# An attention and gated feed-forward kernel whose table of work order is replaced

## The chip, the core and the metric

The kernel runs on one core of a Trainium2 chip. The profile names the core's engines: PE is the matrix engine (PEld its weight loads), DVE the vector engine, ACT the scalar engine with the function tables, POOL the general engine, and SP the queue from which this kernel issues all its DMAs. Each engine works through its own list of instructions in the order in which the kernel wrote them, and waits where an instruction needs something that another engine or a DMA has not finished. The metric is the device time of one execution in microseconds (us). A profiled execution also gives a span, from the first to the last instruction.

## The reference, cut to what matters

Queries, keys and values have shape 4 x 8 x 768 x 64 (batch, heads, positions, head width). Scores are taken inside a narrow window and against one summary per block of 32 keys; the result is turned into 3072 x 512 tokens and goes through a gated feed-forward layer with a cosine gate.

```python
k_sum = k.reshape(B, H, nb, block, D).max(axis=3)      # block 32, nb 24
v_sum = v.reshape(B, H, nb, block, D).mean(axis=3)
scores_l = scale * np.matmul(q, k.transpose(0, 1, 3, 2))       # kept where |i - j| < 16
scores_s = scale * np.einsum('bhsd,bhnd->bhsn', q, k_sum) + np.log(block)
a = softmax(concatenate([scores_l_masked, scores_s]))          # 1e-9 added to the sum
attn = np.matmul(a, concatenate([v, v_sum], axis=2))
x = attn.transpose(0, 2, 1, 3).reshape(B * S, H * D)           # 3072 x 512
h = x @ w_in                                                    # 512 -> 2048
out = (h * np.cos(h)) @ w_out                                   # 2048 -> 512
```

## The kernel before, in words

The tokens are cut into eight blocks of 384 (half of one batch entry). In each block the attention is done for four groups, each a pair of heads; the groups are called a, b, c and d, so that `c3` is the third group of block 3. A group loads q, k and v, turns q and k, takes the largest key of every 32 (`ks`), forms scores on PE (`sc`), copies or scales them out of PSUM (`z`), takes maximum, difference, exponential, sum, reciprocal and product (`mx su ex sm iv nm`), turns the result (`tp` on PE, or `pt` on DVE with a trip through DRAM, `po` and `pi`), and multiplies it with v on PE (`va`). The result is split into a high part and a rest (`xh`, `xl`).

The feed-forward layer runs in 128 steps, `s0` to `s127`. A step takes one of 16 slices of 128 hidden columns for one block. Its up product is 12 matmuls of 384 columns (line 705); then come five short operations on ACT and DVE with one tile `t` (turns L715, residue L718, sine L723, gate L727), a high part `gh` (L344 or L346) and a rest `gl` (L350); its down product is 9 matmuls of 512 columns (line 756), 6 with `gh` and 3 with `gl`, added into three banks of PSUM that the block keeps until its last slice. The tiles `t`, `gh` and `gl` have two buffers each. Block 0 is done in two runs, slices 0 to 5 (s0 to s5) and 6 to 15 (s22 to s31), around the whole of block 1 (s6 to s21). The sixteen weight slices are loaded once and worked into the form that the products need, by ACT, DVE and POOL (`w0` to `w15`: `ab cl sh lb fb hi lo`). The sums over v are formed from loads of their own (`v0_0` to `v3_7`), on POOL or DVE.

What sets the order is a table, `ORDER`: a text of 2118 tokens such as `s4.up.5` or `s0.lo.v`. A token names who works, which operation, and behind that the PSUM banks or staging buffers it uses and the engine that does it (a ACT, v DVE, p POOL). The kernel goes through the table once, and every token writes its instructions to the lists of the engines concerned. No scheduler moves them later; so the order of two tokens matters where they share an engine, and the waits follow from the data.

```python
for token in ORDER.split():
    who, what, *args = token.split(".")
    one = whose[who]
    getattr(one, does[type(one)][what])(*(int(a) if a.isdigit() else eng_of[a] for a in args))
```

Of the kernel before, what the change touches and what calls it, by code (L numbers as in the profile page):

```python
# [28 lines left out]
a0.k a0.tk.1.0 a0.tk.0.1 a0.ks.1 a0.ck.1.a d0.ms.2.3 a0.q d0.k d0.tk.1.0 a0.ks.0 c0.k c0.tk.1.4 c0.ck.1.v a0.ck.0.v  # L29
a0.tq.5 a0.cq.v a0.ms.7.6 c0.tk.0.1 b0.k b0.q b0.tk.0.5 b0.ks.0 c0.ks.0 a0.sc a0.z.0.v b0.tk.1.7 b0.ck.0.v c0.ks.1  # L30
b0.ck.1.v a0.z.1.a a0.mx a0.su d0.tk.0.6 v0_1.l v0_1.h.v b0.tq.5 b0.cq.v c0.q c0.tq.4 c0.cq.a c0.ck.0.a c0.ms.4.1
c0.sc a0.ex c0.z.1.a v0_0.l v0_0.h.p v0_0.s.p c0.v v0_1.s.v d0.ks.1 b0.ks.1 d0.ks.0 a0.sm b0.ms.5.1 b0.sc b0.z.0.v
c0.z.0.v a0.iv c0.mx w1.l w1.ab.0 w1.cl.v w1.sh.4.5 w1.lb w1.fb.1 d0.q d0.tq.7 b0.z.1.a d0.ck.0.a d0.cq.a c0.su c0.ex
c0.sm c0.iv a0.v a0.nm d0.ck.1.a d0.sc a0.tp.1.0 a0.tp.0.1 c0.nm c0.tp.0.4 c0.tp.1.5 b0.mx w1.hi.a w1.lo.p w0.l
w0.ab.0 w0.sh.6.7 w0.cl.v w0.lb c0.m d0.z.0.a d0.z.1.a d0.mx a0.cp.1.a d0.su a0.cp.0.a b0.su w2.l w2.ab.0 w2.sh.0.1
a0.m a0.va.2 w0.fb.1 c0.cp.1.a w0.hi.a w0.lo.p c0.cp.0.a c0.va.3 w2.cl.v w2.lb a0.xh.v d0.ex d0.sm c0.xh.v d0.iv d0.nm
b1.q w5.l w5.sh.4.5 w5.ab.0 b0.ex w2.fb.1 w2.hi.a w2.lo.p d0.m a0.xl a1.ms.6.7 b1.tq.0 b1.cq.a d0.tp.1.2 d0.tp.0.1
d0.cp.1.a d0.cp.0.a c1.q c1.tq.0 w5.cl.v b0.sm w5.lb b0.iv c0.xl b0.nm w3.l a1.q a1.tq.2 a1.cq.a a1.sc w3.ab.0 w5.fb.1
w3.sh.1.2 w3.cl.v w3.lb d0.v a1.z.1.a c1.cq.a a1.z.0.a a1.mx a1.su d0.va.3 d0.xh.a d0.xl c1.ms.4.5 c1.sc c1.z.1.v w4.l
w4.ab.0 w5.hi.v w5.lo.p b0.tp.1.0 c1.z.0.a b0.cp.1.a b1.ms.7.6 w4.sh.3.4 w4.cl.v w4.lb c1.mx c1.su w4.fb.0 b0.tp.0.0  # L40
b0.cp.0.a b1.sc b1.z.1.a b0.v d1.q d1.tq.0 b0.m d1.cq.a b0.va.5 b0.xh.a b0.xl d1.ms.0.6 d1.sc d1.z.1.v a1.ex a1.sm
# [902 lines left out]
```

## Time and profile before

| what | us |
|---|---|
| median of three runs | 658.23 (657.37 to 658.73) |
| the profiled execution, its own time | 658.99 |
| its span | 657.2 |
| PE busy | 635.1 |
| DVE busy | 437.0 |
| ACT busy | 316.7 |
| POOL busy | 247.4 |
| first matmul starts at | 4.70 |
| first up product starts at | 55.88 |

The profiled execution took 0.76 us more than the median, and 1.8 us of it lie outside its span. In rows of a timeline or of the chain of waits the first number is the start after the beginning of the span, the second the time taken; `x12` is a count of instructions. Brackets give the idle time of the engine before that row and what ended it. In rows by stretches of time each engine has busy time and, in brackets, its number of instructions; then stand the granted PE clock as a share of full speed, the busy share of the DMA engines and GB/s.

### The profile page before, as it was taken

The numbers are of one execution on the slowest core, as the hardware profiler recorded it, in microseconds if no ns is written. First come the engines' busy times: TensorE is split into PE (matmuls) and PEld (weight loads), VectorE is DVE, ScalarE is ACT, GpSimd is POOL, SyncE is SP. The second block draws the span as 40 slices with busy tenths as digits, with TensorE's granted clock in tenths as the row PEclk, the third lists the DMA queues.
The fourth block names the chain that finished last, engine by engine and source line by source line (L and its number), as shares of the span: only waits on it lengthen the run. The fifth ranks groups of instructions, "written<-read, shape, count | busy, mean of one in ns | idle before, by whom it ended". The sixth has DMA issues, their size and how long they took to land.

```text
span 657.2 us, 13183 instructions
## 1 busy us (share of the span) xinstructions
PE 635.1 (97%) x5141; PEld 562.7 (86%) x5141; DVE 437.0 (67%) x768; ACT 316.7 (48%) x520; POOL 247.4 (38%) x251
## 2 busy tenths in 40 slices
PE   5679999999999999999999999999999999999996
PEld 4568889888988988898898989889898998899995
DVE  4998999868765667766776856487456675634422
ACT  1698876646553552324555534226433553323232
POOL 3778867465424424012342535115321111301021
PEclk9769999999999999999999999999999999999999
DMA  9997554652334434425444433563124232200001
GB/s 224 289 256 214 155 185 150 194 111 44 85 92 136 121 109 110 116 55 120 106 111 109 130 84 96 123 136 100 47 55 129 81 85 66 75 23 17 32 1 48
DMA packets 167157, 72.67 MB, mean 111 GB/s; under 512 B 136824, under 2 KB 155832, under 8 KB 167096
## 3 DMA queue, kind: packets, MB, share of 16 engines
q1 hardware_dynamic: 167096, 71.84, 41.3%
q8 instruction: 40, 0.66, 0.4%
q14 instruction: 21, 0.17, 0.1%
HBM read 53.72 MB, written 15.73 MB: 106 GB/s over the span
## 4 chain that ended last, share of the span: by engine, by line
PE 88%; DVE 4%; DMA 4%; ACT 1%; SPq 1%; issue 1%; POOL 0%; ACTq 0%; DVEq 0%; POOLq 0%
PE banks L756 38%; PE banks L705 38%; PE banks L560 4%; PE banks L661 4%; PE banks L547 2%; DMA late<-in_moe_w_out_dram 1%; PE banks L617 1%; DMA out_dram<-stage 1%; PE banks L506 1%; DMA late<-in_k_dram 1%; DMA kn<-in_v_dram 1%; SPq L484 0%; DVE t L727 0%; DVE gl L350 0%; PE banks L493 0%
## 5 line engine op out<-in xcount | busy, mean ns | idle before, releaser
L705 PE MATMUL banks<-xh,w 128*128 128x384 f32 x1024 | 278.1, 338 | 1.1 <-DVE stage L406 1.1
L756 PE MATMUL banks<-w,gh 128*128 128x512 f32 x768 | 198.7, 394 | 0.5 <-DVE t L727 0.5
L705 PEld LDWEIGHTS banks<-xh,w 128*128 128x128 f32 x1024 | 186.6, 188 | 6.1 <-DVE stage L406 1.7
L705 PE MATMUL banks<-xl,w 128*128 128x384 f32 x512 | 171.7, 335 | 0.0
L756 PEld LDWEIGHTS banks<-w,gh 128*128 128x128 f32 x768 | 142.5, 188 | 29.0 <-DVE t L727 0.8
L350 POOL TENSOR_TENSOR gl<-t,gh 128x384 fp32r<-128x384 f32 x69 | 70.9, 1031 | 226.5 <-ACT gh L344 99.2
L715 ACT ACTIVATE t<-banks 128x384 int32<-128x384 f32 x128 | 61.9, 489 | 156.9 <-PE banks L705 74.2
L718 DVE SCALAR_TENSOR_TENSOR t<-t,banks 128x384 f32<-128x384 int32 x128 | 69.1, 546 | 75.9 <-ACT t L715 75.8
L723 ACT ACTIVATE t<-t 128x384 f32<-128x384 f32 x128 | 66.3, 524 | 91.4 <-DVE t L718 91.0
L756 PE MATMUL banks<-w,gl 128*128 128x512 f32 x384 | 110.1, 394 | 0.0
L727 DVE TENSOR_TENSOR t<-t,banks 128x384 f32<-128x384 f32 x128 | 69.7, 548 | 48.2 <-ACT t L723 47.2
L705 PEld LDWEIGHTS banks<-xl,w 128*128 128x128 f32 x512 | 96.1, 188 | 2.8
L756 PEld LDWEIGHTS banks<-w,gl 128*128 128x128 f32 x384 | 70.9, 188 | 12.8
L584 POOL TENSOR_TENSOR sc<-sc,m 128x720 f32<-128x720 f32 x28 | 41.2, 1474 | 78.4 <-DVE m L579 78.4
L608 POOL TENSOR_TENSOR sc<-sc,r 128x720 f32<-128x720 f32 x28 | 39.8, 1424 | 42.9 <-DVE r L605 42.0
L344 ACT CAST gh<-t 128x384 fp32r<-128x384 f32 x69 | 34.6, 511 | 32.7 <-DVE t L727 27.3
L350 DVE TENSOR_TENSOR gl<-t,gh 128x384 fp32r<-128x384 f32 x59 | 38.5, 656 | 16.3 <-ACT gh L344 12.0
L350 POOL TENSOR_TENSOR w<-stage,w 128x1024 fp32r<-128x1024 f32 x14 | 34.6, 2471 | 12.0 <-ACT w L344 7.0
L560 PEld LDWEIGHTS banks<-kd,qd 64*64 64x64 f32 x1344 | 27.8, 132 | 6.9 <-issue 3.2
L253 POOL TENSOR_TENSOR kn<-kn 96x256 f32<-96x256 f32 (+1 forms) x32 | 20.0, 625 | 32.1 <-DMA kn<-in_v_dram 16.4
L560 PE MATMUL banks<-kd,qd 64*64 64x24 f32 (+1 forms) x1344 | 30.9, 231 | 0.8 <-ACT qd L499 0.6
L600 DVE TENSOR_REDUCE r<-sc 128x6 f32<-128x726 f32 x28 | 25.2, 899 | 8.0 <-ACT sc L597 7.9
(101 smaller groups left out, 607.8 us busy)
## 6 DMA issues: line engine op xcount, KB each, us to landing
pd<-stage SPq DMA_DIRECT2D x22, 384.0 KB
late<-in_moe_w_in_dram SPq DMA_DIRECT2D x16, 512.0 KB
late<-in_moe_w_out_dram SPq DMA_DIRECT2D x16, 512.0 KB
pt<-pd SPq DMA_DIRECT2D x66, 96.0 KB
vn<-in_v_dram SPq DMA_DIRECT2D x52, 120.0 KB
out_dram<-stage SPq DMA_DIRECT2D x23, 256.0 KB
kn<-in_v_dram SPq DMA_DIRECT2D x24, 192.0 KB
qn<-in_q_dram SPq DMA_DIRECT2D x92, 48.0 KB
```

Source lines behind the costliest of these rows:

```text
L344: eng.copy(out=out, in_=in_)
L350: eng.tensor_tensor(out=lo, in0=src, in1=hi.bitcast(F32), op=ALU.subtract)
L560: nc.tensor.matmul(out=self.sp[hh][s * QT : (s + 1) * QT, c, lo : lo + n], lhsT=self.qd[rows, t * QT : (t + 1) * QT], rhs=self.kd[rows, ke ...
L584: nc.gpsimd.tensor_tensor(out=self.sc, in0=self.sc, in1=self.m.unsqueeze(2).broadcast_to([P, U, NK]), op=ALU.subtract)
L608: nc.gpsimd.tensor_tensor(out=self.sc, in0=self.sc, in1=self.r.unsqueeze(2).broadcast_to([P, U, NK]), op=ALU.mult)
L661: nc.tensor.matmul(out=self.xps[rows, t * QT : (t + 1) * QT], lhsT=self.vn[:, t, rows], rhs=self.pt[2 * c + hh][s], start=True, stop=True,)
L705: nc.tensor.matmul(out=self.h, lhsT=w_of(name, self.f)[:, c * P : (c + 1) * P], rhs=x_of(self.blk, part, c), start=n == 0, stop=n == last,)
L715: nc.scalar.activation(out=self.t.bitcast(I32), in_=self.h, func=AF.Copy, scale=1.0 / TWO_PI, bias=0.25)
L718: nc.vector.scalar_tensor_tensor(out=self.t, in0=self.t.bitcast(I32), scalar=-TWO_PI, in1=self.h, op0=ALU.mult, op1=ALU.add)
L723: nc.scalar.activation(out=self.t, in_=self.t, func=AF.Sin, scale=-1.0, bias=-0.5 * math.pi)
L727: nc.vector.tensor_tensor(out=self.t, in0=self.t, in1=self.h, op=ALU.mult)
L756: nc.tensor.matmul(out=self.acc[i], lhsT=g[:, i * P : (i + 1) * P], rhs=w_of(name, self.f), start=self.first and n == 0, stop=self.last an ...
```

## The change

Only the table `ORDER` is replaced. The new one has the same 2118 operations; a note with it says that loads, sums of v and the changes of the matrix engine between up and down products are counted in it as traced. All functions and all sizes stay. Apart from the places of the tokens, their last parts differ: banks, staging buffers, and for some operations the engine.

```diff
 ORDER = """
-a0.k a0.tk.1.0 a0.tk.0.1 a0.ks.1 a0.ck.1.a d0.ms.2.3 a0.q d0.k d0.tk.1.0 a0.ks.0 c0.k c0.tk.1.4 c0.ck.1.v a0.ck.0.v
-a0.tq.5 a0.cq.v a0.ms.7.6 c0.tk.0.1 b0.k b0.q b0.tk.0.5 b0.ks.0 c0.ks.0 a0.sc a0.z.0.v b0.tk.1.7 b0.ck.0.v c0.ks.1
...
-w12.l v1_3.l v1_3.s.v v1_4.l w6.sh.0.1 s8.tu s8.re s7.hi.v s6.dh.2.3.4 s6.dl w6.cl.p w6.lb w6.fb.1 s5.st.1 w11.l s8.si
...
-s7.dl s10.up.0 s11.up.1 s9.hi.a s8.dh s8.dl s9.dh w12.sh.5.6 s10.tu s9.lo.p s11.tu s11.re s11.si s10.re s10.si w6.lo.p
...
+a0.k a0.tk.0.0 a0.ks.0 a0.ms.1.2 a0.tk.1.3 a0.q d0.k d0.tk.0.4 d0.ck.0.a a0.ck.0.a a0.tq.5 c0.k b0.k b0.tk.1.6
+d0.tk.1.0 a0.cq.v a0.ck.1.v b0.ks.1 d0.ks.1 d0.ks.0 c0.tk.0.7 c0.tk.1.5 c0.ks.1 a0.ks.1 b0.ck.1.v c0.ck.0.a b0.tk.0.4
...
+w6.hi.a s8.si s6.dh.0.1.2 s8.ga s8.hi.v s6.dl s7.dh s7.dl s9.re s9.si w12.ab.0 s8.lo.v s9.ga s9.hi.v s9.lo.v s11.tu
...
```

Counted over the table, the engines that do an operation change as follows.

| operation | before | now |
|---|---|---|
| rest of a step, `gl` | 69 POOL, 59 DVE | 55 POOL, 73 DVE |
| high part of a step, `gh` | 69 ACT, 59 DVE | 60 ACT, 68 DVE |
| rest of a weight slice (`w.lo`) | 14 POOL, 2 DVE | 9 POOL, 7 DVE |
| clamp of a weight slice (`w.cl`) | 3 POOL, 13 DVE | 1 POOL, 15 DVE |
| copy of a turned result (`cp`) | 19 ACT, 1 DVE | 16 ACT, 4 DVE |
| taking a block's results (`ta`) | 12 ACT, 12 DVE | 20 ACT, 4 DVE |

Three places follow as the lists of the engines have them. The first is the beginning of PE's list. Here `late` and `kn` and `x` in line 506 are loaded keys that are turned (`late_127` holds those of a and b, `kn` those of d, `x_2` those of c), line 493 turns a query, line 547 puts a mask into two banks, and line 560 is the first score product of a0. Before:

```order
L506 MATMUL banks<-ident,late_127 128x128 x6
L547 MATMUL banks<-mask,ident 128x360 x2
L506 MATMUL banks<-ident,kn 128x128 x3
L506 MATMUL banks<-ident,x_2_137 128x128 x3
L493 MATMUL banks<-ident,late_128 128x128 x3
L547 MATMUL banks<-mask,ident 128x360 x2
L506 MATMUL banks<-ident,x_2_137 128x128 x3
L506 MATMUL banks<-ident,late_127 128x128 x3
L560 MATMUL banks<-kd_99,qd 64x96
```

And now:

```order
L506 MATMUL banks<-ident,late_127 128x128 x3
L547 MATMUL banks<-mask,ident 128x360 x2
L506 MATMUL banks<-ident,late_127 128x128 x3
L506 MATMUL banks<-ident,kn 128x128 x3
L493 MATMUL banks<-ident,late_128 128x128 x3
L506 MATMUL banks<-ident,late_127 128x128 x3
L506 MATMUL banks<-ident,kn 128x128 x3
L506 MATMUL banks<-ident,x_2_137 128x128 x6
L506 MATMUL banks<-ident,late_127 128x128 x3
L560 MATMUL banks<-kd_99,qd 64x96
```

Ahead of a0's first score product stood both halves of the keys of a and c and one half each of b and d; now all eight halves stand there, and the two masks are one. The list of DVE at the same place (line 527 takes the largest keys, `kd_99` to `kd_102` are the turned keys of a to d, lines 346 and 501 copy keys and queries) was before:

```order
L527 TENSOR_REDUCE kd_99<-banks 128x12 x2
L346 COPY kd_101<-banks 128x384
L346 COPY kd_99<-banks 128x384
L501 TENSOR_SCALAR qd<-banks 128x384
L527 TENSOR_REDUCE kd_100<-banks 128x12
L527 TENSOR_REDUCE kd_101<-banks 128x12
L346 COPY sc<-banks 128x3x120
```

and is now:

```order
L527 TENSOR_REDUCE kd_99<-banks 128x12
L501 TENSOR_SCALAR qd<-banks 128x384
L346 COPY kd_99<-banks 128x384
L527 TENSOR_REDUCE kd_100<-banks 128x12
L527 TENSOR_REDUCE kd_102<-banks 128x12 x2
L527 TENSOR_REDUCE kd_101<-banks 128x12
L527 TENSOR_REDUCE kd_99<-banks 128x12
```

The second of a's two reductions, which a0's scores need, has moved behind one of b, both of d and one of c.

The third place is PE's list at the first down product of block 1, of step s6 (weights `w_436` before, `w_433` now; `xh` and `xl` are the two parts of x). Before, the down product of s6 is followed by the up product of another step:

```order
L756 MATMUL banks<-w_436,gh 128x512 x6
L756 MATMUL banks<-w_436,gl 128x512 x3
L705 MATMUL banks<-xh_1_854,w_758 128x384
L705 MATMUL banks<-xl_1_856,w_758 128x384
L705 MATMUL banks<-xh_1_854,w_758 128x384 x2
L705 MATMUL banks<-xl_1_856,w_758 128x384
L705 MATMUL banks<-xh_1_854,w_758 128x384
```

Now four down products stand in one row, and four up products ahead of them:

```order
L705 MATMUL banks<-xh_1_958,w_699 128x384
L756 MATMUL banks<-w_433,gh 128x512 x6
L756 MATMUL banks<-w_433,gl 128x512 x3
L756 MATMUL banks<-w_397,gh 128x512 x6
L756 MATMUL banks<-w_397,gl 128x512 x3
L756 MATMUL banks<-w_462,gh 128x512 x6
L756 MATMUL banks<-w_462,gl 128x512 x3
L756 MATMUL banks<-w_795,gh 128x512 x6
L756 MATMUL banks<-w_795,gl 128x512 x3
L705 MATMUL banks<-xh_1_857,w_1212 128x384
```

Over the whole list of PE, an up product directly follows a down product 71 times before and 11 times now; a down product directly follows an up product 81 times before and 22 times now. The pieces of attention that stand between feed-forward work are 39 before and 38 now. Runs of down products with no up product among them that are longer than four steps are 1 before (five steps) and 9 now (five to eight steps).

More of the change, by code (lines that the diff above doesn't have):

```diff
@@ L34 @@
[L34 to L38, printed above, removed]
@@ L170 @@
+s127.re s127.si s127.ga s127.hi.v s127.lo.p s126.dh s126.dl s127.dh s127.dl s127.ta.2.a s111.st.0 s127.ta.0.0.v
+s127.st.2 s127.st.0 s127.tb.2.v s127.sb.2 s127.ta.1.1.a s127.st.1
 """
```

268 lines of the change are left out of this document (136 added, 132 removed).

## The prediction

> **What bounds the kernel now.** I read the page first, for the busy shares and the slices, then the stretches of time, then the chain of waits and the timeline of PE where it has gaps.
>
> ```profile
> PE 635.1 (97%) x5141; PEld 562.7 (86%) x5141; DVE 437.0 (67%) x768; ACT 316.7 (48%) x520; POOL 247.4 (38%) x251
> PE   5679999999999999999999999999999999999996
> PEclk9769999999999999999999999999999999999999
> ```
>
> PE is busy for 97% of the span; what it is short of lies in the first three slices and the last, and in slices two and three its clock was lowered.
>
> ```profile
> 0.00:56.00 56.00, 40.78 (x585) 31.08 (x586) 44.91 (x64) 33.86 (x52) 36.02 (x55) 0.85 0.95 251
> 56.00:130.00 74.00, 72.92 (x457) 65.37 (x457) 67.88 (x101) 54.47 (x84) 52.57 (x46) 1.00 0.59 177
> 130.00:652.00 522.00, 521.26 (x4102) 466.27 (x4100) 323.61 (x604) 227.53 (x384) 158.82 (x151) 1.00 0.34 86
> 652.00:657.20 5.20, 0.17 (x1) 0.00 (x0) 0.64 (x2) 0.87 (x2) 0.00 (x0) 0.72 0.42 151
> ```
>
> So four stages. Up to the first up product at about 56 us, PE is idle for 56.00 - 40.78 = 15.2 us; from there to 130 us for 1.1; in the 522 us behind for 0.7; at the end for 5.0, in which the last results are taken and stored. Between 56 and 652 us no wait is left to remove that is worth more than 1.8 us in all. There the new order can only gain from how closely matmuls follow each other, and it can lose wherever PE now waits.
>
> **The change part by part.** All 5141 matmuls stay, so the work of PE stays; its order changes.
>
> *Changes between up and down products.* The chain of waits, whose pieces are PE itself here, prices them:
>
> ```profile
> 92.73 2.10 PE banks L705 x12
> 94.84 2.08 PE banks L756 x9
> 96.92 2.10 PE banks L705 x12
> ...
> 408.08 8.34 PE banks L705 x48
> 416.43 6.84 PE banks L756 x30
> 423.27 2.10 PE banks L705 x12
> 425.37 1.39 PE banks L756 x6
> ```
>
> By the starts, 12 up matmuls between down products take 94.84 - 92.73 = 2.11 us and 48 take 8.35. The 36 more cost 6.24, which is 2.08 for 12: an up piece behind a down piece pays 0.03 beside its matmuls. Likewise 9 down matmuls take 2.08 and 30 take 6.84: 21 more cost 4.76, or 0.227 each, so 9 should cost 2.04 and a piece pays 0.04; the piece of 6 took 1.39 against 1.36, or 0.03, and I give a piece of 3 0.02. Up behind down goes from 71 times to 11: 60 x 0.03 = 1.8 us less. Down behind up goes from 81 (10 pieces of 3 matmuls, 12 of 6, 59 longer) to 22 (all of 18 or more): 0.2 + 0.36 + 2.36 = 2.9 before, 0.9 now, 2.0 less. Together 3.8. The starts are rounded to 0.01, which makes each price uncertain by about 0.005: 120 changes by 0.005 are 0.6, so 3.2 to 4.4. I take 3.6, a little under the middle, since the 0.03 for an up piece rests on the smallest difference.
>
> *Pieces of attention* between feed-forward work cost something too:
>
> ```profile
> 448.25 1.02 PE banks L560 x36
> 449.27 2.29 PE banks L705 x12
> 451.55 2.08 PE banks L756 x9
> ```
>
> Behind scores 12 up matmuls took 451.55 - 449.27 = 2.28, or 0.17 over 2.11. There are 39 such pieces before and 38 now; one fewer is 0.2 us at most, and I leave it out.
>
> *The beginning.* PE's rows up to its last large wait:
>
> ```profile
> 6.01 2.61 PE L547 MATMUL banks<-mask,ident 128*128 128x360 f32 x4
> ...
> 9.79 1.38 PE L547 MATMUL banks<-mask,ident 128*128 128x360 f32 x4
> ...
> 11.32 0.49 PE L506 MATMUL banks<-ident,late 128*128 128x128 f32 x3
> 11.75 1.09 PE L560 MATMUL banks<-kd,qd 64*64 64x96 f32 x48
> ...
> 22.36 1.08 PE L560 MATMUL banks<-kd,late 64*64 64x24 f32 x46 [1.57 <-DVE kd L527]
> 24.06 0.55 PE L493 MATMUL banks<-ident,qn 128*128 128x128 f32 x3 [0.61 <-DMA qn<-in_q_dram]
> 26.88 2.44 PE L560 MATMUL banks<-kd,late 64*64 64x96 f32 x48 [2.27 <-ACT late L499]
> 29.25 1.54 PE L617 MATMUL banks<-ident,sc 128*120 128x128 f32 x6
> 31.31 1.54 PE L617 MATMUL banks<-ident,late 128*120 128x128 f32 x6 [0.52 <-POOL late L608]
> 33.35 1.55 PE L661 MATMUL banks<-pt,vn 120*64 120x64 f32 x24 [0.51 <-ACT pt L344]
> 37.36 1.55 PE L661 MATMUL banks<-pt,x 120*64 120x64 f32 x24 [2.46 <-ACT pt L344]
> ```
>
> and, from the groups by line, DVE's reduction of keys:
>
> ```profile
> L527 DVE TENSOR_REDUCE kd<-banks 128x12 f32<-128x384 f32 x10 | 5.3, 551 | 4.0 <-ACT kd L344 2.2 <-PE banks L506 1.7
> ```
>
> Now a0's scores stand behind b's keys. Those had landed by 11.32 at the latest, when PE turned them without a wait, and their load is again the fifth. From b's first half on, four groups of three transposes stand up to the last of c, at most 0.43 us each by the step from 11.32 to 11.75, and then DVE's reductions of c and a at 0.55 each: 4 x 0.43 + 2 x 0.55 = 2.8. If b's keys land between 10.5 (an estimate, halfway between the rows at 9.79 and 11.32) and 11.3, a0's scores begin at 13.3 to 14.1 instead of 11.75, 1.5 to 2.4 us late. What this holds up is a0's softmax, and with it the transposes that stood at 29.25. But from 20 to 37.4 us PE waited 1.57 + 0.61 + 2.27 + 0.52 + 0.51 + 2.46 = 7.9 us for DVE, a query, ACT and POOL, so there is room to be late in. Against it, c's query is now loaded ahead of b's and of the second load of v; POOL, and no longer DVE, does the halving of v; and the masks and queries of block 1 (`a1.ms`, `b1.tq`, `a1.tq`) now stand ahead of c0's product with v, where PE waited 2.46 us. Queries for d still come behind the first weight slice, so the wait that ended at 24.06 stays. I take the first up product at the same 56 us, with bounds from 3 us earlier (less than half of the 7.9 us removed) to 5.4 later (the third rival).
>
> The lowered clock belongs here. Four masks took 2.61 us at 6.01 and 1.38 at 9.79, so the rate doubled, and later it fell back:
>
> ```profile
> 9.20:26.30 17.10, 11.23 (x184) 7.86 (x182) 15.78 (x24) 5.44 (x9) 8.37 (x8) 1.00 1.09 270
> 26.30:43.30 17.00, 12.93 (x121) 10.55 (x122) 16.00 (x20) 15.47 (x23) 14.77 (x9) 0.50 0.92 275
> ```
>
> Half the clock held for 17 us behind gaps of 0.6 and 2.27 us. The Trainium skill, "TensorE: Matmul & The Clock Gate", section "Part 1: The HAM clock gate", says that the half rate is the default, and that a busy window of some 3.4 us lifts it and an idle one brings it back. By that rule a start with fewer gaps would run 17 us less at half the clock, and one with a gap ahead of a0's scores would stay at it longer; the trace agrees in the rate, but its longest gap there, 2.27 us, is shorter than such a window, so partly idle windows seem to count. The sum would stay at its value by either, unless the gaps move; that is the third rival.
>
> *Waits in the long runs.* A step's `t` comes free when its rest is done, and there are two. The loop without neighbours, from the end of the program:
>
> ```profile
> 642.02 0.49 ACT L715 ACTIVATE t<-banks 128x384 int32<-128x384 f32 x1 [2.10 <-PE banks L705]
> ...
> 646.03 0.49 ACT L715 ACTIVATE t<-banks 128x384 int32<-128x384 f32 x1 [1.18 <-POOL gl L350]
> ```
>
> 646.03 - 642.02 = 4.01 us for every second step, against two down products of PE, 2 x 2.05 = 4.1. Four steps are ready when a run begins (two with `gh` and `gl`, two with `t`), so runs up to four don't feel the loop; a fifth step and those behind it do, with 0.1 us to spare for two steps, and less where attention's work on ACT or DVE falls between. The run of five at the end of the program went through without a gap. I take no more waits than the 1.8 us of now, and keep 0 to 5.4 as bounds (nine long runs with 0.4 each, that is 3.6, on top of 1.8).
>
> *More work on DVE.* Moving `gl` and weight rests to DVE takes it from 67.88 of 74 us in the second stage:
>
> ```profile
> L350 POOL TENSOR_TENSOR w<-stage,w 128x1024 fp32r<-128x1024 f32 x14 | 34.6, 2471 | 12.0 <-ACT w L344 7.0
> L350 DVE TENSOR_TENSOR w<-stage,w 128x1024 fp32r<-128x1024 f32 x2 | 2.4, 1220 | 0.0
> ```
>
> Five more rests at 1.22 are 6.1 us over the sixteen slices, and as much room is left (74 - 67.9). Up to the 16th gate DVE has 166 instructions before and now, because products with v and sums have gone to ACT and POOL in turn. I cost it at nothing; the room hides it, and without that it is part of the bounds above. The end is the same three takes and four stores in another order, and stays at its 5 us.
>
> *The sum.* From the profiled execution, 658.99 - 3.6 = 655.4 us; that execution lay 0.76 over the median, so the median of the new order should be about 654.6.
>
> **The rivals.**
>
> First, a shorter beginning: PE's waits for ACT and DVE at 22 to 37 us shrink, and with them perhaps the stretch at half the clock. For it speaks that block 1's masks and queries now fill c0's wait and that ACT has three copies of `pt` fewer; against it that d's query and the weights land when they did (DMA engines 0.95 busy to 56 us). 3 us less: 651.6.
>
> Second, the long runs starve: nine places at 0.4 us give back the 3.6, and the time is 658.2. For it speaks the loop of 4.01 against 4.1; against it that five steps in a row ran free at the end.
>
> Third, on the other side, the beginning at half the clock: a0's scores wait behind b's keys, the gap ahead of them keeps the clock low, and the 11.23 us of PE work between 9.2 and 26.3 take twice as long. 22.5 us do not fit into 17.1; the first up product comes 5.4 us later, and the time is 654.6 + 5.4 = 660.0. It decides from a first up product after about 60.8 us (55.9, the 3.6 gained, and 1.3). For it speaks that masks of 2.61 us and transposes of twice the time were the state before 9 us; against it that 5.9 us of the stretch were idle and that other chains go on meanwhile.
>
> Fourth, the price of a change is not saved, because the same cost sits elsewhere, as at the ends of accumulations, which stay: 658.2. Against it speaks that pieces of 48 and 30 contain such ends and don't show it.
>
> **How the numbers follow.** The forecast has a chance of 0.43, the shorter beginning 0.19, starving runs 0.14, the slow beginning 0.16 and no saving 0.08. The likeliest case alone spans 652.5 to 656.8. A measurement of this kernel can tell about 0.2%, or 1.3 us, from no change: faster is under 656.9, slower over 659.5. Faster gets 0.43 + 0.19 = 0.62, the same 0.14 + 0.08 = 0.22, with 0.02 of it given to slower for runs that starve longer: 0.20, and slower 0.18. The range of 650.0 to 660.3 reaches over the first rival and just over the third; left out are a beginning shorter by over 4.6 us and several losses at once, together under 0.2.
>
> **What would show each step right or wrong.** In the new profile's chain, pieces of 36 to 72 up matmuls at 2.08 us for 12 and of 27 or more down matmuls at 0.227 each show the saving; stretches such as 130 to the end of PE's work would be shorter by about 3 us with the same waits. The start of the first up product, 55.88 now, tells the beginning's part directly, with the granted clock of its slices. Gaps ahead of line 756 inside runs, released by `gh` or `gl`, would show starving; gaps ahead of line 705 released by a weight slice would show DVE too full. The forecast is wrong if the first up product moves by over 2 us, or if PE is idle for over 4 us between it and its last matmul.

## The result and the profile after

The new order takes 653.91 us in the median of four runs (653.28 to 655.12), against 658.48 us before (657.37 to 659.19, four runs). The ratio is 0.9935, with an interval from 0.9919 to 0.9951: 4.6 us faster, where 3.6 were forecast. The profiled execution took 654.17 us, with a span of 652.4 against 657.2, so the two traces differ by 4.8 us, and these can be placed.

From the page of the new kernel, the busy times and the granted clock by 40 slices:

```profile
PE 630.4 (97%) x5141; PEld 558.6 (86%) x5141; DVE 450.3 (69%) x797; ACT 304.1 (47%) x503; POOL 216.0 (33%) x234
PEclk9789999999999999999999999999999999999999
```

The same 5141 matmuls keep PE busy 4.7 us less; DVE has 13.3 us more. By stretches of time (columns as before: busy time of PE, PEld, DVE, ACT and POOL, then granted clock, DMA share, GB/s):

```profile
0.00:56.00 56.00, 40.24 (x593) 30.01 (x594) 45.70 (x67) 33.32 (x53) 33.75 (x51) 0.91 0.93 249
56.00:130.00 74.00, 74.00 (x470) 67.56 (x469) 67.29 (x104) 53.48 (x82) 44.66 (x50) 1.00 0.58 177
130.00:647.00 517.00, 515.71 (x4080) 461.01 (x4079) 336.73 (x627) 216.39 (x368) 137.56 (x135) 1.00 0.34 87
647.00:652.40 5.40, 0.40 (x2) 0.00 (x0) 0.62 (x2) 0.87 (x2) 0.00 (x0) 0.78 0.40 146
```

PE waits for 1.29 us between 56 and 647 us (517.00 - 515.71), where it waited for 1.8 before, and for 5.0 at the end, as before. The beginning, by PE's timeline:

```profile
10.72 0.52 PE L506 MATMUL banks<-ident,late 128*128 128x128 f32 x3 [1.64 <-DMA late<-in_k_dram]
...
13.29 1.53 PE L560 MATMUL banks<-kd,qd 64*64 64x96 f32 x48
...
22.31 1.86 PE L560 MATMUL banks<-kd,late 64*64 64x96 f32 x48 [2.35 <-DVE late L501]
...
33.70 1.01 PE L661 MATMUL banks<-pt,vn 120*64 120x64 f32 x24 [2.09 <-DMA vn<-vs]
...
35.94 1.48 PE L547 MATMUL banks<-mask,ident 128*128 128x360 f32 x4 [0.54 <-DVE stage L406]
38.89 0.77 PE L493 MATMUL banks<-ident,late 128*128 128x128 f32 x3 [1.47 <-ACT pt L344]
39.59 1.55 PE L661 MATMUL banks<-pt,x 120*64 120x64 f32 x24
...
44.07 1.38 PE L547 MATMUL banks<-mask,ident 128*128 128x360 f32 x4
...
54.35 0.45 PE L705 MATMUL banks<-xh,w 128*128 128x384 f32 x1
```

The keys of b landed at 10.72 and a0's scores began at 13.29, as forecast; yet the first up product starts at 54.35 instead of 55.81. (The prediction's 55.88 was the end of what stands ahead of it; from here on starts of matmuls are compared.) So 1.5 of the 4.8 us between these two traces come from the beginning. From there to the end of the last matmul it is 593.05 us instead of 596.36, which is the other 3.3.

The two parts don't stand equally firm. The stretch behind the first up product repeats: in four runs below that leave it alone (e3, e7, e8, e9) it is 592.7 to 593.4 us, and in two with the order before (e6, e12) 595.6 and 597.8. The beginning doesn't: four runs below (e1, e2, e5, e11) have the new order's beginning unchanged, and their first up products start at 56.43, 54.34, 54.37 and 54.58. The same lists can thus differ by 2.1 us there, more than the 1.5, which rest on one trace of each kernel.

Long pieces in the chain of waits look as expected:

```profile
240.04 10.42 PE banks L705 x60
250.46 8.20 PE banks L756 x36
```

60 ups take 10.42, or 2.08 for twelve, and 36 downs 0.228 each. The 593 and 596 us can be summed over the steps from one matmul's start to the next. Idle time is counted by itself; of what is left of a step, an up product has 0.1733 us and a down product 0.2267 us, the same sum in both kernels, and what goes beyond that is sorted. Steps that go beyond by 0.08 us or more (by 0.1 us as a rule) are called slow steps.

```
                                                     before   after   difference
first ten matmuls of an up or down piece that
  stands directly behind one of the other kind,
  without slow steps                                  4.42     1.18      -3.24
slow steps at the ends of pieces (75 and 65)          7.86     6.69      -1.17
slow steps inside pieces (0 and 16)                   0.00     2.00      +2.00
PE's idle time                                        1.81     1.29      -0.52
products of attention                                53.88    53.16      -0.72
the rest                                              0.87     1.20      +0.33
together                                                                 -3.3
```

The first row is the price of changes, forecast at 3.6. It is steady: 4.42 and 4.41 in e6 and e12, which have the order before behind the first up product, and 1.16 to 1.18 in e3, e7, e8 and e9, which have the new one.

### The profile page after: what moved, and what is told of

Read it like the earlier page. It is cut to its first block, busy times and chain, and to the rows that moved or that the text cites. A ratio compares the mean times of both kernels' runs of the same rounds, so it can differ in the third digit from the quotient of the medians.

```text
span 652.4 us, 13154 instructions
## 1 busy us (share of the span) xinstructions
PE 630.4 (97%) x5141; PEld 558.6 (86%) x5141; DVE 450.3 (69%) x797; ACT 304.1 (47%) x503; POOL 216.0 (33%) x234
## 4 chain that ended last, share of the span: by engine, by line
PE 88%; DVE 6%; ACT 1%; issue 1%; SPq 1%; POOL 1%; DMA 1%; ACTq 0%; DVEq 0%
PE banks L705 40%; PE banks L756 38%; PE banks L560 4%; PE banks L661 4%; PE banks L617 1%; SPq L447 1%; POOL w L350 1%; DVE kd L527 1%; DMA late<-in_k_dram 1%; PE banks L547 1%; DVE stage L406 1%; DVE vs L263 1%; DVE m L579 1%; DVE t L727 0%; DVE t L718 0%
## 5 line engine op out<-in xcount | busy, mean ns | idle before, releaser
L705 PE MATMUL banks<-xh,w 128*128 128x384 f32 x1024 | 268.6, 337 | 0.1
L350 POOL TENSOR_TENSOR gl<-t,gh 128x384 fp32r<-128x384 f32 x55 | 57.3, 1043 | 223.9 <-DVE gh L346 107.6
L718 DVE SCALAR_TENSOR_TENSOR t<-t,banks 128x384 f32<-128x384 int32 x128 | 69.4, 546 | 67.0 <-ACT t L715 66.3
L584 POOL TENSOR_TENSOR sc<-sc,m 128x720 f32<-128x720 f32 x28 | 39.2, 1403 | 72.4 <-DVE m L579 70.3
L350 DVE TENSOR_TENSOR gl<-t,gh 128x384 fp32r<-128x384 f32 x73 | 45.0, 620 | 16.7 <-ACT gh L344 10.4
L344 ACT CAST gh<-t 128x384 fp32r<-128x384 f32 x60 | 30.7, 511 | 39.5 <-DVE t L727 28.2
L346 DVE CAST gh<-t 128x384 fp32r<-128x384 f32 x68 | 28.3, 417 | 15.7 <-PE banks L756 12.4
L597 ACT ACTIVATE sc<-sc 128x720 f32<-128x720 f32 x28 | 22.5, 805 | 27.4 <-POOL sc L584 27.3
L253 POOL TENSOR_TENSOR kn<-kn 96x256 f32<-96x256 f32 (+1 forms) x36 | 23.3, 647 | 32.0 <-DMA kn<-in_v_dram 23.6
```

Source lines behind the costliest of these rows:

```text
L344: eng.copy(out=out, in_=in_)
L346: eng.tensor_copy(out=out, in_=in_)
L350: eng.tensor_tensor(out=lo, in0=src, in1=hi.bitcast(F32), op=ALU.subtract)
L584: nc.gpsimd.tensor_tensor(out=self.sc, in0=self.sc, in1=self.m.unsqueeze(2).broadcast_to([P, U, NK]), op=ALU.subtract)
L705: nc.tensor.matmul(out=self.h, lhsT=w_of(name, self.f)[:, c * P : (c + 1) * P], rhs=x_of(self.blk, part, c), start=n == 0, stop=n == last,)
L718: nc.vector.scalar_tensor_tensor(out=self.t, in0=self.t.bitcast(I32), scalar=-TWO_PI, in1=self.h, op0=ALU.mult, op1=ALU.add)
```

## The experiments

The kernel before ran again beside each group of experiments, with medians of 658.60 to 659.36 us, and the ratios are against those runs. The new order didn't; times over its 653.91 us are therefore sure to about 1 us only.

**1. Changes put back (e1_alternate).** At 14 places of the new order where a step's 12 up matmuls stand ahead of a step's six early down matmuls, the two alternate, two ups and one down. That adds 140 changes and moves nothing else.

```diff
+        def up_with_down(self, i, d, *banks):
+            ...
+            for n, (c, name, part) in enumerate(ups):
+                nc.tensor.matmul(...)                      # the up product as in up()
+                if n % 2 and n // 2 < len(downs):
+                    d.products([downs[n // 2]])
```

> The changed kernel, in which at 14 places an up product is followed by the first 6 matmuls of a down product; here these 18 matmuls alternate, two of up and one of down. That adds 140 changes between up and down (33 to 173) and no matmul. If every change costs 0.03 to 0.04 us whatever the length of the pieces, as the prediction has it: 140 x 0.035 = 4.9 us more than the changed kernel's 653.9, so about 658.8. If the cost is a slower rhythm of the first six to nine matmuls behind a change (their starts lie 0.176 to 0.181 apart instead of 0.173 for up and 0.231 to 0.236 instead of 0.227 for down): 14 x (12 x 0.005 + 6 x 0.006) = 1.3 us, so about 655.2. If a change costs nothing and the gain came from waits: 653.9.

Measured: 657.05 us (655.85 to 659.00), ratio 0.9972 [0.9957, 0.9987] against before. Its profiled execution had a slower beginning (first up product at 56.43; why, is looked at under 5), so only the stretch from there to the last matmul is compared; by stretches, this kernel and then the new order:

```profile
56.40:652.30 595.90, 593.06 (x4565) 530.88 (x4557) 406.03 (x733) 271.31 (x452) 181.83 (x184) 1.00 0.37 98
```

```profile
54.35:647.40 593.05, 591.76 (x4561) 530.22 (x4557) 405.66 (x733) 271.51 (x451) 182.56 (x184) 1.00 0.37 98
```

PE is idle for 2.84 us in the one and 1.29 in the other. Of 2.75 us by starts (595.80 against 593.05), 1.55 are thus waits, and 1.2 are left for 140 changes: 0.009 each at most. At 0.03 to 0.04 each they would have cost 4.2 to 5.6. Changes that follow each other after one or two matmuls are far cheaper than the prediction's price; whether the price itself fell, this run couldn't say.

**2. The price by itself (e5_price).** Behind the last token stand blocks of matmuls that wait for nothing and whose results nobody uses.

```diff
+            for piece in (48, 24, 12, 6, 3, 1):
+                for n in range(192):
+                    one_down(DM) if n // piece % 2 else one_up(0, self.f)
+            for piece in (48, 6):                          # downs of 384 columns
+                for n in range(192):
+                    one_down(TB) if n // piece % 2 else one_up(0, self.f)
+            for piece in (48, 6):                          # ups only, two banks and slices
+                for n in range(192):
+                    one_up(n // piece % 2, self.f - n // piece % 2)
```

> The new order, and behind its last token matmuls whose results nobody uses: six blocks of 96 up and 96 down products in pieces of 48, 24, 12, 6, 3 and 1 (3, 7, 15, 31, 63 and 191 changes inside a block); then 96 ups and 96 downs of only 384 columns in pieces of 48 and of 6; then 192 ups in pieces of 48 and of 6 that alternate between two banks and two weight slices. Nothing waits inside the blocks, so each block's length tells the price of a change by itself. The base is 96 x 0.1733 + 96 x 0.2267 = 38.40 us. Price of the prediction, 0.03 to 0.04 for each change whatever the piece: 38.5, 38.6, 38.9, 39.5, 40.6 and 45.1 us. A slower rhythm of the first 9 matmuls behind a change (0.004 us each) and nothing else: 38.5, 38.7, 39.0, 39.2, 39.2 and 39.2. If the different widths cause it, the pair of blocks with 384 columns on both sides shows no difference between pieces of 48 and 6, and the last pair neither; if it is the change of tensors or banks, both pairs show one of 0.4 to 1.0.

Measured in its one execution, from the starts of the matmuls: 38.62, 38.67, 38.93, 38.96, 39.15 and 39.04 us for pieces of 48, 24, 12, 6, 3 and 1, and 33.28 in all four of the other blocks. In its chain of waits (L718 the ups, L726 the downs; start, length, matmuls):

```profile
666.99 8.34 PE banks L718 x48
675.33 10.92 PE banks L726 x48
686.26 4.18 PE banks L718 x24
...
724.92 2.10 PE banks L718 x12
727.03 2.76 PE banks L726 x12
729.79 2.10 PE banks L718 x12
...
766.31 1.04 PE banks L718 x6
767.35 1.39 PE banks L726 x6
768.74 1.04 PE banks L718 x6
...
914.28 1.04 PE banks L718 x6
915.32 1.04 PE banks L726 x6
916.36 1.04 PE banks L718 x6
```

A pair of 48 takes 686.26 - 666.99 = 19.27, or 0.07 over 48 x 0.4; a pair of 12 takes 4.87, again 0.07 over 4.80; a pair of 6 takes 2.43, or 0.03 over 2.40. So an isolated pair of changes costs 0.07, which is the prediction's 0.03 + 0.04. But it isn't paid at the change. It is a slower rhythm of the matmuls behind it, by a few ns each up to about the sixth up and the ninth down, so shorter pieces pay only for the matmuls that they have, and 191 changes in single matmuls cost 0.6 us in all, not 5.7 more than none. Downs of 384 columns in pieces of 6 show nothing (914.28 to 916.36 is 2.08 = 12 x 0.1733), nor does a change of bank and weights alone. So here the price hangs on the two widths, 384 and 512 columns. Why a change of width slows the next matmuls, no run shows.

**3. Shorter pieces by later ups (e2_late_ups).** 54 up products of the new order were moved later, one place of many shown by PE's tokens, so that direct changes rise from 33 to 96.

```diff
-... s11.up.6 s9.up.7 s8.up.4 s10.up.3 s6.dh.0.1.2 s6.dl s7.dh s7.dl ...
+... s9.up.7 s8.up.4 s6.dh.0.1.2 s6.dl s11.up.6 s10.up.3 s7.dh s7.dl ...
```

> The changed kernel with part of the grouping undone: 54 up products stand later in PE's list, behind down products, as far as two pieces of PE's work stay between them and their own turns; everything else stays. Direct changes between up and down go from 33 to 96. With the price of the prediction: 33 x 0.03 + 30 x 0.035 = 2.0 us more, so 655.9, and PE's idle time as it was. If the grouping saved waits and no change costs: the pieces keep their time (12 up matmuls 2.08 us, 9 down 2.04) and only idle time grows. If grouping was worth nothing: 653.9.

Measured: 722.2 us (719.8 to 723.7), ratio 1.0954 [1.0927, 1.0981]. By what PE waited for (total, times, longest) between 56 and 717 us:

```profile
PE banks L756 <- DVE gh L346: 9.0, 8, 2.8
...
PE banks L705 <- DVE t L727: 5.0, 4, 1.7
PE banks L756 <- ACT gh L344: 4.7, 1, 4.7
```

Over 40 us of waits, and the mean granted clock from 130 us on fell to 0.97. The theory that pieces differ only by the price of their changes fell by far. An up product that starts early also starts the chain turns, residue, sine, gate, high part that its down product needs. The long pieces of the new order work because each run of ups stands ahead of the run of downs that it feeds.

**4. How near the long runs are to starving (e11_rests_pool).** All 73 rests `gl` on DVE go to POOL.

```diff
-... s1.lo.v ... s2.lo.v ...
+... s1.lo.p ... s2.lo.p ...
```

> The new order with all 128 rests gl on POOL (73 of them were on DVE; 1.02 us each there instead of 0.56). It lengthens the loop by which a tile t comes free by 0.46 us for more than half of the steps. Theory of the prediction, a loop of 4.01 us against 4.1 for two steps leaves 0.1: the long runs of down products starve, by 0.2 to 0.3 us for each of some 20 steps behind the fourth of a run, PE idle 4 to 7 us more between the first up and the last down product, time 3 to 7 over the new order's. Rival, steps are far enough ahead: idle as in the new order (1.3 us), time within 0.7.

Measured: 668.03 us (667.09 to 669.37), ratio 1.0141 [1.0119, 1.0163], 14 us over the new order; from the first up product (54.58) to the last matmul it is 605.74 us, 12.7 more. The direction is that of the prediction's theory, but not the place. From PE's timeline and POOL's:

```profile
119.52 1.65 PE L756 MATMUL banks<-w,gl 128*128 128x512 f32 x3 [4.10 <-POOL gl L350]
```

```profile
115.54 1.24 POOL L253 TENSOR_TENSOR kn<-kn 96x256 f32<-96x256 f32 x2 [2.75 <-DMA kn<-in_v_dram]
...
117.53 1.94 POOL L350 TENSOR_TENSOR gl<-t,gh 128x384 fp32r<-128x384 f32 x2
```

Eight pauses of 0.37 to 4.27 us make 10.6 of the 12.7, all within the first four steps of runs of at most four steps, save one of 0.79 in the third step of the run of eight. The largest is a queue: the rest stands on POOL behind a sum of v that waited 2.75 us for its load. In the other eight long runs no pause is over 0.14 us: in the run of seven that begins at 610.4, the starts of 63 matmuls span 14.09 us, where 62 x 0.2267 = 14.05 are the least. So a rest that takes 0.46 us more doesn't starve a long run, and the prediction's loop, with 0.1 us to spare and a cost from the fifth step on, isn't what limits them. Something else may help the long runs here: DVE is busy for 410.3 us instead of 450.3, so its own parts of the loop come sooner. Why there is more room than the loop at the program's end suggested stays open. What more rests on DVE spare is the queue behind POOL's other work.

**5. What sets the beginning: the clock? (e3_fill, e6_before_fill, e7_after_fill2, e9_after_fill3.)** Idle mask products fill PE's waits, so that the clock stays full. In the new order 23 of them (e3), then eleven in shorter fills (e7, e9); in the order before, six (e6).

```diff
+        def fill(self, i, n):
+            for _ in range(n):
+                nc.tensor.matmul(
+                    out=bank(i)[:, : QC * NK].rearrange("p (c n) -> p c n", c=QC), lhsT=ident,
+                    rhs=mask[:, self.half : self.half + QC, :], start=True, stop=True,
+                )
```

> The changed kernel with 23 added matmuls (identity times mask, into banks that are free, never read) at four places of the beginning where PE waited: ahead of b0's scores, of the first turn of a0's result, of a0's product with v, and of the turn of b1's query. They keep PE busy and change no other work. If the lowered clock (22.0 to 28.8 and 39.1 to 42.5 us) costs: it stays at full, the pieces of PE between them take half (about 4 us less of PE time) and the first up product comes 1 to 2.5 us earlier than 54.35, the time 651.4 to 652.9. If the beginning is set by loads, DVE, ACT and POOL: the clock stays full but the first up product stays within 0.4 us and the time at 653.9. If the fillers come in the way: later than 54.35 by up to 2 us.

> The order before, with three idle mask products ahead of d0's scores and three ahead of c0's product with v, in the two largest waits of PE's beginning (2.27 and 2.46 us); they go to a bank that is overwritten. Theory that before's 17 us at half the clock made its beginning longer: the clock stays full up to c0's product with v at about 37.4, and the 18.45 us of work behind it, of which 5.98 ran at half the clock, shrink by 3.0: first up product at 52.8 to 53.5 instead of 55.81, time 2.3 to 3.0 under before. Rival, the beginning is set by the loads and the weights' preparation, and the clock only fills waits: first up product at 55.5 to 56.5, time within 1 us of before.

> The new order with eleven idle mask products in four waits of PE's beginning (3 ahead of b0's scores, 3 ahead of a0's first turn of weights, 3 ahead of a0's product with v, 2 ahead of the query of a1 that waits for c0), about half as many as in the run with 23, where the fillers outlasted the waits by 1 to 1.6 us. Theory that the clock lengthens the work behind the last wait: from that query on 13.5 us at the full clock instead of 15.5, first up product at 52.4 to 53.2, time 1.2 to 2.0 under the new order's. Rival, loads and other engines set the first up product: 54 to 55, time within 0.7 of the new order's.

> As the run with eleven fillers, but the last two stand ahead of the masks of a1 and in a bank of those masks, so that they wait for nothing that the masks don't wait for (there they had waited 3.29 us for the clamp of a weight slice). Theory that the lowered clock lengthens PE's work behind its last wait: clock full from 9 us on, first up product at 52.4 to 53.4 instead of 54.35, time 1.0 to 2.0 under the new order's 653.9. Rival, the clock costs only what waits hide: first up product at 54.0 to 55.0, time within 0.7 of the new order's.

Measured: e3 654.85 us, ratio 0.9935 [0.9921, 0.9950], first up product at 55.03; e6 658.29, ratio 1.0001 [0.9980, 1.0022], at 56.30; e7 658.44, ratio 0.9998 [0.9983, 1.0014], at 58.25; e9 654.63, ratio 0.9946 [0.9927, 0.9965], at 54.53. In the new order two stretches run at half the clock, and in e9 none does; by stretches, first the new order:

```profile
22.00:28.80 6.80, 4.82 (x57) 3.89 (x57) 6.72 (x11) 3.94 (x6) 3.75 (x3) 0.50 0.89 250
...
39.10:42.40 3.30, 3.16 (x32) 2.44 (x31) 3.01 (x6) 3.17 (x6) 2.24 (x3) 0.50 0.88 235
```

```profile
10.50:56.00 45.50, 38.09 (x596) 27.17 (x595) 44.27 (x62) 31.59 (x50) 29.17 (x17) 1.00 0.97 260
```

What e9 won on PE came back as waits that had been covered; from its timeline:

```profile
40.93 0.62 PE L624 MATMUL banks<-ident,late 128*120 128x128 f32 x4 [0.99 <-DVE late L501]
...
51.85 0.52 PE L493 MATMUL banks<-ident,qn 128*128 128x128 f32 x3 [0.62 <-DMA qn<-in_q_dram]
...
54.53 0.44 PE L712 MATMUL banks<-xh,w 128*128 128x384 f32 x1
```

The clock was full in e9 and the first up product didn't come earlier. In e6 half the clock held for 6.8 us instead of 17, and again nothing was gained. These runs show that filling the waits doesn't pay; they don't show that the lower clock is free, for the fillers stand in PE's list too. In e6 c0's product began at 38.79 instead of 37.36.

e1 tells more. Up to 96 us its lists are those of the new order, and in its trace the wait for `pt` that ended at 38.89 in the new order ended at 38.95. From its timeline behind that:

```profile
41.33 1.59 PE L617 MATMUL banks<-ident,late 128*120 128x128 f32 x6 [0.99 <-DVE late L501]
...
45.33 2.52 PE L547 MATMUL banks<-mask,ident 128*128 128x360 f32 x4
...
56.43 0.44 PE L705 MATMUL banks<-xh,w 128*128 128x384 f32 x1
```

Half the clock held here from 40.81 to 47.64, in the new order's trace from 39.07 to 42.49. The masks that took 1.38 us there took 2.52, and the first up product came 2.1 us later. PE waits for nothing behind 41.33 in either trace, so the clock alone is left to make the difference. Half the clock costs nothing where it only fills a wait: in the new order's trace it took the place of the 0.99 us that PE waits for DVE in e1 and e9. Where no such wait is left, it is paid. How much of the new beginning's 1.5 us is the clock, whose 17 us at half had become 10, these runs don't tell. Over the 70 executions of the kernel before that ran beside the experiments, the clock and the time go together: the 15 with a mean clock of 0.989 or more have a median span of 655.9 us, the 24 with 0.984 or less 658.3. Which of the two follows from the other, or both from a third, that doesn't say.

The Trainium skill, "TensorE: Matmul & The Clock Gate", section "Part 1: The HAM clock gate", says that windows of some 3.4 us decide, and the lengths at half the clock agree (3.41, 6.83 and 17.07 us are one, two and five of them).

In e7 the last two fillers went to a bank that a weight slice still used, and PE waited for DVE:

```profile
40.74 2.77 PE L553 MATMUL banks<-mask,ident 128*128 128x360 f32 x4 [3.29 <-DVE stage L406]
```

The first up product was 3.9 us late, and the time is 4.5 over the new order's. So a delay on PE's list at this place is paid, while a gain there may not be kept.

**6. The order of the beginning (e8_masks_behind, e4_a0first, e12_before_mask_first, e10_two_masks_less).** e8 undoes one part of the change: the masks of a1 and the queries of b1 and a1 stand behind c0's product with v again.

```diff
-... b1.tq.5 d0.nm ... a1.ms.6.7 w2.fb.1 b1.cq.v ... a1.tq.2 a1.cq.a ... c0.va.4 d0.m ...
+... c0.va.4 b1.tq.5 b1.cq.v a1.ms.6.7 a1.tq.2 a1.cq.a d0.m ...
```

> The new order with one part of its beginning undone: the masks of a1 and the queries of b1 and a1 stand behind c0's product with v again, as in the order before. Theory that this move is worth the work it takes out from behind the last wait (1.48 + 0.33 + 0.33 at the full clock): first up product 1.5 to 2.5 later than 54.35, at 55.8 to 56.9, time 1.5 to 2.5 over the new order's. Rival, the beginning's gain is all clock, or is set elsewhere: first up product at 54 to 55, time within 0.7 of the new order's.

Measured: 655.75 us (655.09 to 656.46), ratio 0.9959 [0.9943, 0.9975], 1.8 us over the new order:

```profile
39.04 1.55 PE L661 MATMUL banks<-pt,x 120*64 120x64 f32 x24 [2.25 <-ACT pt L344]
...
41.21 2.61 PE L547 MATMUL banks<-mask,ident 128*128 128x360 f32 x4
...
56.66 0.45 PE L705 MATMUL banks<-xh,w 128*128 128x384 f32 x1
```

c0's product begins half a microsecond earlier than in the new order (39.04 against 39.59), but the masks and queries now stand behind it: first up product at 56.66, 2.3 later than in the new order's trace and 0.85 later than in that of the kernel before. That is the work that was moved, but not alone: half the clock held here until 44.14, and the masks took 2.61 us instead of 1.48. Six executions are 1.6 us slower than the new order by the ratios (0.9959 against 0.9935), at the edge of what the two intervals can tell apart. So this part of the new order is worth 1.6 us by the times and 2.3 by the traces; that the beginning would have become longer without it, one trace doesn't show.

e4 undoes another part: a0's scores stand ahead of b's keys again.

```diff
-... b0.tk.1.6 d0.tk.1.0 ... b0.ks.0 c0.ks.0 a0.sc c0.ms.3.5 ... a0.z.0.a ... a0.mx ...
+... a0.ks.1 a0.sc b0.tk.1.6 d0.tk.1.0 ... c0.ks.1 a0.z.0.a a0.z.1.v a0.mx ...
```

> The changed kernel with a0's scores put back ahead of b's keys on PE, and the largest keys of a, the copies of a0's scores and its maximum moved forward with them on DVE. PE's wait of 1.64 us for b's keys no longer stands ahead of a0's scores, which should start near 9.8 instead of 13.29 us. If that lateness was hidden, as the prediction has it: first up product within 0.5 us of 54.35, time 653.4 to 654.4. If it set the beginning: 1.5 to 2.4 us earlier, 651.5 to 652.4. If the clock stays low longer because PE is now idle elsewhere: later.

Measured: 655.83 us (654.88 to 658.26), ratio 0.9947 [0.9927, 0.9967]. The scores began at 9.58 instead of 13.29, and the first up product came at 56.52. (The traced execution is the slowest of the six, and half the clock held in it from 38.52 to 45.35.) Starting a0's scores 3.7 us earlier gained nothing: none of the six executions is under the new order's median. So what holds them up was rightly called hidden.

e12 does one part alone in the order before: only the masks of a1 go ahead of c0's product with v.

```diff
-... c0.va.3 ... a0.xl a1.ms.6.7 b1.tq.0 ...
+... a1.ms.6.7 c0.va.3 ... a0.xl b1.tq.0 ...
```

> The order before with one thing of the new one: the masks of a1 (2.77 us at half the clock, at 38.85) stand ahead of c0's product with v, in PE's wait of 2.46 us that ended at 37.36. The bank that they need comes free at 35.28, by the second DVE operation L406 of that stretch (34.06 + 1.22), so they fill that wait from there to 38.05, 0.7 over its end. Theory that PE's work behind the wait sets the first up product: 2.77 - 0.69 = 2.1 us earlier, at 53.2 to 54.5 instead of 55.81, time 1.3 to 2.5 under before. Rival, that DVE and the weights set it (as where two masks fell away and half of it came back as waits): first up product earlier by under 1 us or with new waits of 1 us and more right behind it, time within 0.8 of before.

Measured: 660.67 us (657.3 to 662.51), ratio 1.0022 [1.0003, 1.0041], 1.5 over before. The rival's new wait came, but its time missed too.

```profile
35.69 2.77 PE L547 MATMUL banks<-mask,ident 128*128 128x360 f32 x4
38.39 1.06 PE L661 MATMUL banks<-pt,x 120*64 120x64 f32 x24
41.31 0.55 PE L493 MATMUL banks<-ident,late 128*128 128x128 f32 x3 [1.86 <-DVE stage L406]
...
57.79 0.45 PE L705 MATMUL banks<-xh,w 128*128 128x384 f32 x1
```

The masks filled the wait as worked out, but the query behind them (`b1.tq.0`) then waited 1.86 us for DVE: its bank 0 is that of the weight slice `w2.sh.0.1`, and the masks had covered that wait before. Half the clock held for 20.5 us, the last 6.8 of them from 42.16, behind PE's last large wait. In the new table that query has bank 5. So in the order before the move alone doesn't pay, and the bank was in its way; the move with the other bank was not run there.

e10 asks whether less PE work behind the last wait is worth its length: b1 and d1 get their masks from DVE, as the blocks behind do.

```diff
-MASKS = "11111111000000000000000000000000"
+MASKS = "11111010000000000000000000000000"
-... b1.ms.4.3 b1.sc ... b1.z.1.a ... d1.ms.3.4 d1.sc ...
+... b1.sc.4.3 ... b1.z.1.v ... d1.sc.3.4 ...
```

> The new order; for b1 and d1 the mask is no longer put into PSUM by PE but added by DVE when it takes the scores, as the groups of blocks 2 to 7 do it: eight records of mask products (1.31 + 1.41 us by the steps of the timeline) fall away on PE behind its last wait, and one take goes from ACT to DVE (about 0.5 us). Theory that PE's own work behind the last wait sets the first up product: 51.5 to 52.2 instead of 54.35, time 2.0 to 2.9 under the new order's 653.9. Rival, that the weights or DVE (9.6 of 10 us busy there) set it: first up product at 53.8 to 54.9 with a wait of PE in front or right behind, time within 0.7.

Measured: 655.41 us (654.4 to 656.47), ratio 0.9949 [0.9931, 0.9967], no gain over the new order (0.9935 [0.9919, 0.9951]).

```profile
49.90 0.92 PE L661 MATMUL banks<-pt,vn 120*64 120x64 f32 x24 [1.18 <-ACT pt L344]
...
52.88 0.44 PE L705 MATMUL banks<-xh,w 128*128 128x384 f32 x1
...
54.43 0.44 PE L705 MATMUL banks<-xl,w 128*128 128x384 f32 x1 [0.59 <-DVE xl L350]
```

The first up product came 1.47 earlier, half of the 2.7; 1.18 us went into a wait for ACT ahead of it, and from it to the last matmul it is 595.70 us instead of 593.05, with waits for DVE and ACT behind it. From 36 to 76 us DVE is busy for 39.0 of 40 us here, ACT for 34.3 and PE for 33.6, so an earlier first up product isn't by itself an earlier end. Of all orders tried here none was faster than the new one.

## Why the prediction was right, and where it was not

**Time and range.** 653.91 against 654.6, in the range and in the forecast's own range. The profiled execution's 4.8 us are 3.3 in the long stretch and 1.5 in the beginning; the forecast had 3.6 and 0. The 3.3 are borne out by other traces; the 1.5 lie within what the same beginning differs by.

**Changes between up and down products: right, a little over.** The prices held when measured by themselves (0.07 for an isolated pair of changes). In place the slower rhythm fell by 3.24 us, against the 3.6 taken and the bounds of 3.2 to 4.4. That the stretch as a whole gained about as much is in part luck: 2.0 us came back as slow steps inside long pieces, and 1.2 at the ends of pieces, 0.7 in attention and 0.5 of idle time went, none of which the sum had. The fourth rival, no saving, is out. What the prediction didn't see is that the price lies on the matmuls behind a change: it multiplied a price by a count, which holds here since nearly all pieces were long enough to pay in full, and fails in e1.

**Waits in the long runs: right in size, not in the loop behind it.** 1.29 us, where no more than 1.8 was taken. The five largest pauses inside pieces are 0.44 to 0.22 us, four of them waits for `gh` or `gl`; half of the 2.0 us of slow steps stand beside these four. The second rival's nine times 0.4 didn't come, though a smaller cost of its kind did. But the reason given for their bounds, a loop of `t` with 0.1 us to spare from the fifth step on, fell: with all rests on POOL eight of the nine long runs went through with no pause over 0.14 us (e11).

**DVE: right.** Between 56 and 130 us it was busy for 67.29 of 74 us, and PE waited for nothing there. The room wasn't needed: of the 6.1 us that were to fill it nothing shows in this stretch, where 67.88 stood before; the 13.3 us more lie behind it.

**The beginning: taken as unchanged, shorter by 1.5.** The forecast of a0's scores (13.3 to 14.1) held at 13.29, and that their delay is hidden was borne out by e4. The weak step is the sum at its end, "I take the first up product at the same 56 us": it named the masks and queries that fill c0's wait, but didn't price them. Undoing that part costs 1.6 us by the times of e8 and 2.3 at its first up product, some of it by the clock. The 1.5 that remain in the two traces are less than the 2.1 by which the same beginning differed in e1, so whether the beginning gained, and how much, stays open. It is at most the first rival's mechanism at half its 3 us, beside the forecast and not in place of it. The 1.5 is within the 2 us that the prediction set as its limit. The wait for d's query, which the prediction kept, isn't in the new trace.

**The slow beginning.** The third rival's clock did change, but the other way, 10 us at half instead of 17. Filling PE's waits to keep the clock full gained nothing (e3, e6, e9), but e1 shows that half the clock behind the last wait makes the first up product late, which is the third rival's mechanism at a place that it didn't name.

**The end** stayed at 5.0 us.

## What to carry to other kernels

Before pricing a change of kind on an engine, measure whether the price sits at the change or on the work behind it; long pieces pay it once, and single alternations hardly at all. Longer pieces pay only if the producer side runs ahead of them, so look first at what its operations queue behind on their own engines. Where another engine is nearly full (DVE, 39.0 of 40 us in e10), time won on one engine alone is given back. And before reading 1 or 2 us out of two traces, look by how much traces with the same instructions differ there: here it was 2.1 us.

## What the runs showed of the hardware

Up products of 384 columns follow each other every 0.1733 us, downs of 512 every 0.2267. A change between the two widths slows the next six to nine matmuls by a few ns each, and a change of bank, weights and tensors at one width costs nothing (33.28 us in all four blocks). This hadn't been expected.

The traces also show when the clock changes. Cut into stretches of 3.41 us from one change of the clock to the next, up to the last matmul, the fourteen traces have 29 after which it fell to half, with PE busy in them for 1.66 us or less, and 2672 after which it stayed full, all but two with 1.68 us or more (those two 1.52 and 1.65). It rose again after the 29 stretches at half in which PE was busy for 2.98 us or more, and stayed at half after the 24 with 2.90 or less. The rule quoted in the prediction asks for an idle stretch; here one that was half idle was enough. In e1 the stretch from 40.81 had 2.90 and in the new order's trace that from 39.07 had 3.28, which fits that one stayed at half for a second stretch and the other not.

In e10 one clamp of a weight slice on DVE took 2.95 us, where those beside it took 0.68, while POOL worked on the rest of another slice; from the timelines of DVE and POOL:

```profile
60.14 2.95 DVE L387 TENSOR_SCALAR stage<-stage 128x1024 f32<-128x1024 f32 x1
```

```profile
60.14 2.40 POOL L350 TENSOR_TENSOR w<-stage,w 128x1024 fp32r<-128x1024 f32 x1
```

Both start together, and the clamp ends 0.55 us behind POOL's instruction, as if DVE had stood still for the whole of it. Other clamps on DVE that began while a TENSOR_TENSOR of POOL ran show the same: at 30.82 and 120.94 before and at 35.80 in the new order they took 0.98, 1.42 and 0.98 us and ended 0.55 us behind POOL's instruction. One that began first, at 25.39 before, took 0.68, and POOL's instruction from 25.56 took 1.76 where others like it took 1.39. The Trainium skill, "SBUF — State Buffer", section "SBUF: two separate sides", describes this: certain DVE instructions and GpSimd's (POOL's) share a pair of ports that one of them holds for its whole instruction. These traces agree in the size; no run here tells the port from another cause.
